# Moving group 1's transposes ahead of group 0's masks, group 4's transpose and group 5's loads ahead of the output weights, and tile 1's casts and masks to other steps

## The chip, the cores and the metric

The kernel runs on one core of one Trainium2 chip. The metric is the time of one execution on the device in microseconds (us), the median over the runs. Smaller is better. Profiled spans are some 1.7 us shorter than the time of the same run (236.5 for a run of 238.22).

With one core there is no second die to compare with. A run is called slow here only when it lies more than 1.5% above the fastest run of the same kernel, and ratios leave such runs out. The kernel before has such runs, and they turn out to matter, so below I give the whole spread too.

## The reference, cut to what matters

Causal linear attention with a decay per head, in blocks, then a gated feed-forward layer on its result:

```python
# per block of the sequence, state kv carried from block to block
intra = (q_b @ k_b^T) * Dmask          # scores, masked with the decay
out_b = intra @ v_b + (q_b * lam_pow) @ kv
kv    = lam_block * kv + (k_b * rev_pow)^T @ v_b
# then, on x = out of shape (3072, 512):
y = (silu(x @ w_gate) * (x @ w_val)) @ w_out     # d_ff = 1536
```

The kernel handles the 3072 rows as 12 groups of 256 rows, two groups to a tile of 512. A group is one batch element and two blocks of 128. Groups 0 to 3 are the first blocks of the four batch elements, groups 4 to 7 the next.

## The kernel before

TensorE's order is written by hand as a list of *steps* (one step is one chunk of 128 of the 1536 feed-forward columns: four gate matmuls, four value matmuls), and other work is attached behind a step with `at(step, ...)`. In the timelines of this case GpSimd and VectorE take their instructions in the order of the program. After the change, below, GpSimd's state sum starts at 68.45, just when the v scaling of another group ahead of it ends. In the profile before, VectorE's last mask of group 4 starts at 69.06, right behind a gating product for which VectorE sat idle 2.40 us, though the scores it masks had ended by 63.61. That is the point on which this case turns: an instruction attached early held up what stood behind it on its engine.

```python
def cast_scaled(g, eng=nc.vector):
    ...
    nc.scalar.copy(out=t[:, 0]..., in_=st[("kraw", g)]...)             # L238, ScalarE
    eng.tensor_tensor(out=t[:, 1]..., in0=st[("qraw", g)]..., in1=qd)  # L240, VectorE
    dma_transpose(g)                # L231: one DMA on the load queue, waits for both
def v_scale(g, eng, ...):           # L218, GpSimd
    eng.tensor_tensor(out=st[("vs", g)]..., in0=st[("v", g)]..., in1=rev)
def wo_cast():                      # L212, GpSimd: two of the twelve output-weight chunks
    nc.gpsimd.tensor_copy(out=o, in_=t)
def state(g):                       # L370, L374, L376, GpSimd
    ...                             # kvf = kvl + update; kvz = cast(kvf); kvl = kvf * lamblk
def inter(g, first):                # L386, TensorE: reads kvz
    for r in range(2): ...          # its second half needs state(g)
def ahead(g):
    upd(g)                          # update matmuls, their copy, state(g)
    scores(g)                       # L308; the masks follow on VectorE (L315)
```

The second tile's plan, cut to what moves (tile 1 holds groups 2 and 3; `s1a`: the steps on its first half, the rows of group 2; `s1b`: those on the rows of group 3; `s1c`: the last step, on all 512 rows. `core` is the rest of a group's attention: intra product, inter product and the copy of the result to `xt`):

```python
at(s0["11b"], load_group, 4, "v")
for c in range(0, FC, 2):
    at(s0["11b"], wo_piece, c, c + 2)          # six loads of output weights
...
at(s1a[9], core, 3, SPLIT)                     # intra + inter + evacuation of group 3
at(s1a[9], wo_cast); at(s1a[9], wo_cast)
at(s1a[10], cast_scaled, 4); at(s1a[10], load_group, 5)
...                                            # four more wo_cast at s1b[0], s1b[2]
at(s1b[8], ahead, 4); at(s1b[9], ffn_out, 0, 0)
at(s1b[10], cast_scaled, 5); at(s1b[10], v_scale, 5, nc.gpsimd)
at(s1b[10], load_group, 6)
at(s1b[10], core, 4); at(s1b[10], ffn_out, 0, 1)
at(s1c, ahead, 5); at(s1c, ffn_out, 0, 2); at(s1c, core, 5); at(s1c, ffn_out, 0, 3)
```

In the profile lines below, `qkt` is a group's transposed q and k, `ssb` its masked scores, `v_s` its scaled v, `kvf` and `kvz` the attention state, `woraw` and `wo_sb` the output weights as loaded and as cast, `xt` the attention result that the feed-forward part reads. On TensorE L308 is the scores, L338 the update, L401 the intra and L386 the inter product, L438 and L445 the gate and value matmuls, L460 the output blocks (two lines further down in e_warm from L386 on). "Start to start" means from the start of one group of matmuls to the start of the next; what lies beyond the usual spacing of the two is counted as a wait.

## Time and profile before

| | before |
|---|---|
| median of the first runs | 235.75 us (234.77 to 236.21) |
| the profiled run | 238.22 us, span 236.5 |
| TensorE busy | 224.0 us, 95% |
| waits of TensorE of some 1 us or more after the prologue | four, all between 50 and 96 us |

The median here is of the three runs known when the prediction was made; the fourth, 236.00, puts it at 235.88 further down. One line of this table deserves a second look before the prediction is read: the profiled run is 2.5 us longer than the median of the others. The prediction counts waits in that profile and takes them off the median.

On that profile's page one slice of TensorE's clock stands at 7 tenths: from 76.97 to 80.38, for 3.41 us, the granted clock is 0.50. Such a stretch is meant where a *window* at half clock is spoken of, in the recorded texts too.

### The profile page before, as it was taken

To read this page: it belongs to the slowest core of one execution; us is meant where nothing else is said; L and a number is where in the kernel's file an instruction comes from. 1 tells how busy PE (TensorE), PEld (TensorE's weight loads), DVE (VectorE), ACT (ScalarE), POOL (GpSimd) and SP (SyncE) were. 2 spreads that over 40 slices of the span, in tenths; PEclk is the share of its full clock that TensorE was granted. 3 is DMA by queue.
4 is the path that set the end of the run, shared out by engine and by line. 5 is a ranking of instruction groups with operands and counts; after the bars stand their busy time and mean duration, and the time that the engine had idled before them with its cause. 6 is when DMAs were issued, how large, how long until landed. Compare 5 with 4: busy or idle time off the path is not lost.

```text
span 236.5 us, 5408 instructions
## 1 busy us (share of the span) xinstructions
PE 224.0 (95%) x2215; PEld 122.6 (52%) x2228; DVE 105.0 (44%) x186; ACT 105.1 (44%) x203; POOL 80.0 (34%) x116
## 2 busy tenths in 40 slices
PE   7899999989986898999999999999999999999994
PEld 3566456868853444455454454454454444444443
DVE  5654887567553413546346245255263232232200
ACT  5878586646444053336254254263243344223311
POOL 4667775736992530836532032041020000000000
PEclk9999999999999799999999999999999999999999
DMA  6999999897945926777872924914101001101122
GB/s 201 345 336 362 358 314 312 214 375 252 231 139 139 261 91 170 234 186 217 209 237 72 295 79 71 309 69 101 44 35 44 37 10 46 44 3 44 44 89 89
DMA packets 71018, 39.66 MB, mean 168 GB/s; under 512 B 20178, under 2 KB 66514, under 8 KB 70994
## 3 DMA queue, kind: packets, MB, share of 16 engines
q1 hardware_dynamic: 66482, 32.64, 48.8%
q10 hardware_dynamic: 4512, 6.69, 8.1%
q8 instruction: 17, 0.28, 0.5%
q14 instruction: 7, 0.06, 0.1%
HBM read 28.31 MB, written 6.29 MB: 146 GB/s over the span
## 4 chain that ended last, share of the span: by engine, by line
PE 87%; DMA 6%; DVE 2%; ACT 2%; issue 1%; ACTq 0%; SPq 0%; DVEq 0%
PE bank L460 26%; PE bank L438 25%; PE bank L445 25%; DMA qkt<-qk 4%; PE bank L308 3%; PE bank L401 3%; PE bank L386 2%; DMA kraw<-in_k_dram 1%; DVE ssb L315 1%; PE bank L269 1%; PE bank L338 1%; PE bank L149 1%; ACT xt L412 0%; ACT sil L442 0%; DVE xt L412 0%
## 5 line engine op out<-in xcount | busy, mean ns | idle before, releaser
L448 DVE TENSOR_TENSOR h<-sil,bank 128x512 bf16<-128x512 bf16 (+1 forms) x86 | 51.2, 599 | 105.3 <-PE bank L445 95.7
L438 PE MATMUL bank<-xt,wg_sb 128*128 128x512 bf16 (+1 forms) x344 | 76.5, 345 | 1.6 <-DVE ssb L315 1.0
L445 PE MATMUL bank<-xt,wv_sb 128*128 128x512 bf16 (+1 forms) x344 | 76.3, 344 | 0.0
L442 ACT ACTIVATE sil<-bank 128x512 bf16<-128x512 f32 (+1 forms) x86 | 45.4, 530 | 49.2 <-PE bank L438 46.3
L460 PE MATMUL bank<-wo_sb,h 128*128 128x512 bf16 (+1 forms) x287 | 65.4, 373 | 1.0 <-issue 0.4
L445 PEld LDWEIGHTS <-wv_sb 128*128 128x128 bf16 x344 | 33.7, 98 | 28.8 <-issue 0.2
L438 PEld LDWEIGHTS <-wg_sb 128*128 128x128 bf16 x344 | 32.5, 98 | 29.6 <-issue 1.2
L460 PEld LDWEIGHTS <-h 128*128 128x128 bf16 x300 | 29.4, 99 | 33.2 <-issue 1.5
L462 ACT COPY osb<-bank 128x512 f32<-128x512 f32 (+1 forms) x24 | 13.9, 577 | 60.1 <-PE bank L460 60.1
L370 POOL TENSOR_TENSOR kvf<-kvl,ups 128x256 f32<-128x256 f32 x16 | 11.6, 728 | 67.3 <-ACT ups L360 66.7
L315 DVE TENSOR_TENSOR ssb<-bank,mask 128x512 bf16<-128x512 f32 x40 | 26.1, 685 | 7.7 <-PE bank L308 7.6
L218 POOL TENSOR_TENSOR v_s<-v,rev 128x1024 bf16<-128x1024 f32 (+1 forms) x14 | 23.8, 1704 | 9.9 <-DMA v<-in_v_dram 6.0
L412 ACT CAST xt<-bank 128x512 bf16<-128x512 f32 x21 | 14.4, 737 | 9.1 <-PE bank L401 7.8
L374 POOL CAST kvz<-kvf 64x256 bf16<-64x256 f32 x32 | 13.7, 427 | 1.7
L308 PE MATMUL bank<-qkt 64*64 64x128 bf16 x384 | 9.7, 234 | 4.1 <-DMA qkt<-qk 3.5
L240 DVE TENSOR_TENSOR qk<-qraw,qd 128x1024 bf16<-128x1024 f32 x8 | 11.6, 1455 | 0.0
L308 PEld LDWEIGHTS <-qkt 64*64 64x64 bf16 x384 | 6.9, 114 | 6.6 <-DMA qkt<-qk 3.7
L401 PE MATMUL bank<-ssb,v_s 64*64 64x128 bf16 x384 | 8.6, 227 | 1.1 <-DVE ssb L315 1.1
L238 ACT CAST qk<-kraw 128x1024 bf16<-128x1024 f32 x9 | 9.4, 1039 | 0.0
L212 POOL CAST wo_sb<-woraw 128x1024 bf16<-128x1024 f32 x6 | 6.9, 1159 | 7.0 <-DMA woraw<-in_moe_w_out_dram 7.0
L201 POOL CAST wv_sb<-wraw 128x512 bf16<-128x512 f32 (+1 forms) x9 | 6.8, 754 | 3.9 <-DMA wraw<-in_moe_w_val_dram 3.9
L401 PEld LDWEIGHTS <-v_s 64*64 64x64 bf16 x384 | 6.3, 111 | 3.3 <-issue 2.5
(57 smaller groups left out, 104.7 us busy)
## 6 DMA issues: line engine op xcount, KB each, us to landing
out_dram<-osb ACTq DMA_DIRECT2D x23, 256.0 KB, 2.1
kraw<-in_k_dram SPq DMA_DIRECT2D x10, 512.0 KB, 5.5
qraw<-in_q_dram SPq DMA_DIRECT2D x10, 512.0 KB, 6.0
v<-in_v_dram SPq DMA_DIRECT2D x10, 512.0 KB, 6.6
woraw<-in_moe_w_out_dram SPq DMA_DIRECT2D x6, 512.0 KB, 8.7
wraw<-in_moe_w_gate_dram SPq DMA_DIRECT2D x6, 256.0 KB, 5.5
wraw<-in_moe_w_val_dram SPq DMA_DIRECT2D x6, 256.0 KB, 5.0
wraw<-in_moe_w_gate_dram SPq DMA_DIRECT2D x3, 512.0 KB, 6.8
```

What stands on the lines that cost most here:

```text
L218: eng.tensor_tensor(out=st[("vs", g)][:, h0:h1], in0=st[("v", g)][:, h0:h1].rearrange("p h (s d) -> p h s d", s=2), in1=bap(rev, [[2, h1 - ...
L308: nc.tensor.matmul(sp[(c, h2)][b2 * M:b2 * M + M, n:n + BLK], tt[dp, 0, s, hp, b2 * M:b2 * M + M], tt[dp, 1, :, hp, b2 * M:b2 * M + M], st ...
L315: nc.vector.tensor_tensor(out=ssb[:, h2, 2 * c:2 * c + 2].rearrange("p a s n -> p a (s n)"), in0=sp[(c, h2)].rearrange("p (a x) -> p a x", ...
L374: nc.gpsimd.tensor_copy(out=kvz[b][(i + 1) % 2 if r else 2][dp, :, h2, :], in_=kv[dp])
L401: nc.tensor.matmul(op[r][h2 * 64:h2 * 64 + 64, hp * BLK:hp * BLK + BLK], v_s[ps, 2 * hp + h2, s], ssb[ps, h2, hp, s], start=((first or (i ...
L412: fns[r](out=xt[:, g % 2, :, r].rearrange("p h (m s) -> p h s m", s=2), in_=op[r].rearrange("p (h s m) -> p h s m", h=HP, s=2))
L438: nc.tensor.matmul(gp[:, 0:N], wg_sb[:, mc, fs], xt[:, b0 // 2:b1 // 2, mc].rearrange("p g b n -> p g (b n)"), start=(mc == 0), stop=(mc = ...
L442: nc.scalar.activation(sil[:, 0:N], gp[:, 0:N], AF.Silu)
L445: nc.tensor.matmul(vp[:, 0:N], wv_sb[:, mc, fs], xt[:, b0 // 2:b1 // 2, mc].rearrange("p g b n -> p g (b n)"), start=(mc == 0), stop=(mc = ...
L448: nc.vector.tensor_tensor(out=h_sb[:, fc, b0:b1].rearrange("p b n -> p (b n)"), in0=sil[:, 0:N], in1=vp[:, 0:N], op=ALU.mult)
L460: nc.tensor.matmul(ps, h_sb[:, fc, b], wo_sb[:, fc, c0:c1], start=(fc == 0), stop=(fc == FC - 1))
L462: fn(out=osb[:, c0:c1], in_=ps)
```

## The change

Its intent: have every DMA transpose and every load out before TensorE needs its result, and fill the latency of the prologue. The diff, cut to its core:

```diff
 # prologue (cut): two groups interleaved, more dummy matmuls
-    scores(0, (0,), 1)
+    scores(0, (0,), 3)
 ...
+    cast_half(1, 0, (POOLC, DVEC))          # group 1, ahead of group 0's masks
     run_later(2)
     upd_mm(0, up)
+    ring[0] = 4
+    pe_transpose(1, 0)                      # ahead of group 0's intra product
 ...
 # tile 1
-    for c in range(0, FC, 2):
-        at(s0["11b"], wo_piece, c, c + 2)
-    at(s1a[6], scores, 3)
-    at(s1a[9], core, 3, SPLIT)
-    at(s1a[10], cast_scaled, 4)
-    at(s1a[10], load_group, 5)
-    ... six wo_cast at s1a[9], s1b[0], s1b[2]; v_scale 4 at s1b[1]; state 3 at s1b[3]
-    at(s1b[8], ahead, 4)
-    at(s1b[9], ffn_out, 0, 0)
-    at(s1b[10], cast_scaled, 5); v_scale 5; load_group 6
+    at(s1a[3], cast_scaled, 4)
+    at(s1a[3], load_group, 5)
+    for c in range(0, FC, 2):
+        at(s1a[3], wo_piece, c, c + 2)      # now behind group 4's transpose and group 5
+    at(s1a[6], scores, 3, (0,))
+    at(s1a[7], scores, 3, (1,))
+    at(s1a[10], core, 3, SPLIT); v_scale 4; state 3
+    at(s1b[4], cast_scaled, 5); load_group 6
+    for j in (4, 5, 6):
+        at(s1b[j], wo_cast); at(s1b[j], wo_cast)
+    at(s1b[6], v_scale, 5, nc.gpsimd)
+    at(s1b[7], ahead, 4)                    # its state(4) now behind all of these on GpSimd
     at(s1b[10], core, 4)
+    s1c: ffn_out 0 0, ahead 5, ffn_out 0 1, ffn_out 0 2, core 5, cast_scaled 6, load_group 7, v_scale 6
```

More of the change, by code (lines that the diff above doesn't have):

```diff
@@ L491, in _body @@
     w_piece(4, 6)
-    cast_half(0, 0, (ACTC, DVEC))
+    cast_half(0, 0, (None, DVEC))
     nc.scalar.activation(cinvt, lnp, AF.Exp, scale=-float(BLK))
-    nc.scalar.activation(rev, rev, AF.Exp)
     qdec_table(0)
     qdec_table(1)
+    cast_half(0, 0, (ACTC, None))
+    nc.scalar.activation(rev, rev, AF.Exp)
+    nc.scalar.activation(qd, qd, AF.Exp)
+    nc.scalar.activation(cinv, ln_lam, AF.Exp, scale=-float(BLK))
+    nc.scalar.activation(lamblk, lnp, AF.Exp, scale=float(BLK))
     cast_half(0, 1, (None, DVEC))
@@ L508, in _body @@
     run_later(1)
-    scores(0, (1,), 2)
-    nc.scalar.activation(qd, qd, AF.Exp)
-    nc.scalar.activation(cinv, ln_lam, AF.Exp, scale=-float(BLK))
-    nc.scalar.activation(lamblk, lnp, AF.Exp, scale=float(BLK))
+    scores(0, (1,), 3)
     nc.scalar.preload_act_table_set("silu_and_others")
+    cast_half(1, 0, (POOLC, DVEC))
     run_later(2)
@@ L517, in _body @@
     upd_mm(0, up)
+    ring[0] = 4
+    pe_transpose(1, 0)
     upd_copy(0, (0,))
-    cast_half(1, 0, (POOLC, DVEC))
     cast_half(1, 1, (POOLC, DVEC))
+    ring[0] = 2
     st[("op", 0)] = [bank() for _ in range(2)]
-    warm_into(st[("op", 0)][0], 2)
+    warm_into(st[("op", 0)][0], 3)
     intra(0, True)
-    pe_transpose(1, 0)
-    inter(0, False)
-    pe_transpose(1, 1)
-    upd_copy(0, (1,))
     ring[0] = 4
     scores(1, (0,), 1)
-    scores(1, (1,), 2)
+    run_later(1)
+    ring[0] = 6
+    pe_transpose(1, 1)
+    inter(0, False)
+    run_later(1)
+    upd_copy(0, (1,))
+    ring[0] = 6
+    scores(1, (1,), 3)
     evac(0, (ACTC, None))
@@ L533, in _body @@
     v_scale(1, nc.gpsimd, H // 2, H)
-    run_later(4)
+    run_later(2)
     ring[0] = 0
@@ L607, in _body @@
     s1c = step(1, FC - 1)
-    at(s1a[6], scores, 3)
-    at(s1a[6], upd_mm, 3)
-    at(s1a[6], upd_copy, 3)
-    at(s1a[6], run_later, 2)
-    at(s1a[9], core, 3, SPLIT)
-    at(s1a[9], wo_cast)
-    at(s1a[9], wo_cast)
-    at(s1a[10], cast_scaled, 4)
-    at(s1a[10], load_group, 5)
-    at(s1b[0], wo_cast)
-    at(s1b[0], wo_cast)
-    at(s1b[1], v_scale, 4, nc.gpsimd)
-    at(s1b[2], wo_cast)
-    at(s1b[2], wo_cast)
-    at(s1b[3], state, 3)
-    at(s1b[8], ahead, 4)
-    at(s1b[9], ffn_out, 0, 0)
-    at(s1b[10], cast_scaled, 5)
-    at(s1b[10], v_scale, 5, nc.gpsimd)
-    at(s1b[10], load_group, 6)
+    at(s1a[3], cast_scaled, 4)
[4 more added lines that the diff above has]
+    at(s1a[7], scores, 3, (1,))
+    at(s1a[7], upd_mm, 3)
+    at(s1a[7], upd_copy, 3)
+    at(s1a[10], core, 3, SPLIT)
+    at(s1a[10], v_scale, 4, nc.gpsimd)
+    at(s1a[10], state, 3)
+    at(s1b[4], cast_scaled, 5)
+    at(s1b[4], load_group, 6)
+    for j in (4, 5, 6):
+        at(s1b[j], wo_cast)
+        at(s1b[j], wo_cast)
+    at(s1b[6], v_scale, 5, nc.gpsimd)
+    at(s1b[7], ahead, 4)
     at(s1b[10], core, 4)
-    at(s1b[10], ffn_out, 0, 1)
+    at(s1c, ffn_out, 0, 0)
     at(s1c, ahead, 5)
+    at(s1c, run_later, 3)
+    at(s1c, ffn_out, 0, 1)
     at(s1c, ffn_out, 0, 2)
     at(s1c, core, 5)
+    at(s1c, cast_scaled, 6)
+    at(s1c, load_group, 7)
+    at(s1c, v_scale, 6, nc.gpsimd)
     at(s1c, ffn_out, 0, 3)
@@ L638, in _body @@
         if t == 2:
-            at(sn[0], cast_scaled, 6)
-            at(sn[0], v_scale, 6, nc.gpsimd)
-            at(sn[0], load_group, 7)
             at(sn[2], ahead, 6)
```

## The prediction

> **What bounds the kernel now.** I read the page first, then the chain of waits in order of time, then the timelines of TensorE, GpSimd and the load queue where that chain leaves TensorE. The page and its slices:
>
> ```profile
> span 236.5 us, 5408 instructions
> ...
> PE 224.0 (95%) x2215; PEld 122.6 (52%) x2228; DVE 105.0 (44%) x186; ACT 105.1 (44%) x203; POOL 80.0 (34%) x116
> ...
> PEclk9999999999999799999999999999999999999999
> ...
> PE 87%; DMA 6%; DVE 2%; ACT 2%; issue 1%; ACTq 0%; SPq 0%; DVEq 0%
> ```
>
> TensorE sets the end: 95% busy, 87% of the chain. Nothing makes its matmuls cheaper here, so only its waits can be won, plus the slice where its clock fell to 7 tenths. After 100 us it is busy for 132.68 of 136.5 us (the view of stretches), so the waits lie before. The chain names two:
>
> ```profile
> 72.43 4.95 DMA qkt<-qk
> 77.43 1.07 PE bank L308 x30
> ...
> 89.67 5.38 DMA qkt<-qk
> 95.09 0.64 PE bank L308 x32
> ```
>
> The scores of groups 5 and 6 wait for a DMA transpose that was issued five microseconds before they needed it. The first also leaves TensorE at half speed: the same 32 matmuls take 1.07 us instead of 0.64. TensorE's timeline has the sizes (in brackets: idle time and what ended it):
>
> ```profile
> 51.86 0.60 PE L438 MATMUL bank<-xt,wg_sb 128*128 128x256 bf16 x4 [1.01 <-DVE ssb L315]
> ...
> 69.79 0.41 PE L401 MATMUL bank<-ssb,v_s 64*64 64x128 bf16 x15 [0.90 <-DVE ssb L315]
> ...
> 77.43 1.07 PE L308 MATMUL bank<-qkt 64*64 64x128 bf16 x32 [2.42 <-DMA qkt<-qk]
> ...
> 95.09 0.64 PE L308 MATMUL bank<-qkt 64*64 64x128 bf16 x32 [1.09 <-DMA qkt<-qk]
> ```
>
> Measured from start to start, beyond the usual spacing, they cost: masks of group 3, 1.35 (1.18 + 0.17); masks of group 4, 1.45 (1.10 + 0.35); transpose of group 5, 2.6 plus 1.5 for some 3 us at half clock; transpose of group 6, 1.3. Together 8.2 us, all in tile 1 and at the start of tile 2.
>
> GpSimd is in program order and feeds the attention state:
>
> ```profile
> 60.70 1.03 POOL L212 CAST wo_sb<-woraw 128x1024 bf16<-128x1024 f32 x1
> ...
> 64.66 0.72 POOL L370 TENSOR_TENSOR kvf<-kvl,ups 128x256 f32<-128x256 f32 x1
> 65.44 0.83 POOL L374 CAST kvz<-kvf 64x256 bf16<-64x256 f32 x2
> ```
>
> The last cast of the output weights ends at 61.7; group 4's state is ready at 66.3, and the inter-block product that reads it starts at 67.9. The margin is 1.6 us, and the weights had been requested since 45.25:
>
> ```profile
> 42.88 1.70 SPq L231 DMA_TRANSPOSE qkt<-qk  x1
> 44.63 0.57 SPq L92 DMA_DIRECT2D v<-in_v_dram  x1
> 45.25 3.69 SPq L207 DMA_DIRECT2D woraw<-in_moe_w_out_dram  x6
> ```
>
> The prologue (TensorE's first gate matmul is at 17.3) is latency-bound:
>
> ```profile
> 11.28 0.98 PE bank L401 x30
> ...
> 15.39 1.29 DVE ssb L315 x2
> ```
>
> Group 1's masks end at 16.7, and ScalarE's evacuation of group 0 ends at 17.25. Both end just before the first gate matmul, so shortening one alone gains nothing.
>
> [...] the loads issued behind the transpose of 89.67 land at 96.8, 98.3 and 99.8.
>
> **The change part by part** (minus is a gain; times on the scale of the kernel before).
>
> *Prologue, −0.6.* Group 1's first transposes and casts go ahead of group 0's last masks and intra product; scores and masks of the two groups interleave; four small exponentials move to where ScalarE waits for data; dummy matmuls go from 1+2+2+1+2 to 3+3+3+1+3. VectorE still does eight masks (0.62 each) and the same casts. Followed engine by engine with the row durations: at full clock from about 9 us on, group 1's second transposes end near 12.3 instead of 13.3, the state copies at 13.8, ScalarE's last evacuation of group 0 at 16.0, gate matmuls at 16.0: −1.3. If the clock rises only at 12.1 as now, the eight extra transposes (0.86 at half clock) and three dummies (0.63) stand before the intra product, and the evacuation ends at 17.3: 0. I take about half. Weight casts allow it: the second piece ends at 16.8 on GpSimd, needed at 16.9.
>
> *Scores and core of group 3, +1.0.* The scores come in two halves, one step apart, their masks behind each step's gating product. The second step after reuses the first half's banks: a wait of 0.75; two steps on, the second half's: 0.6. And the core moves from the step before last of the first half-tile to the last one, directly ahead of the step that reads its result: 0.95 for one evacuation (0.73 plus two handovers), which a step of 0.87 covers now. 2.3 against 1.35.
>
> *Transposes of groups 5 and 6, −2.6 −1.5 −1.3.* Group 5's casts and transpose come about six 0.87 us steps earlier, group 6's ahead of the last output block of tile 0. With some 5 us to landing, both are in before their scores. The half-clock stretch goes too.
>
> *Group 4's state, −1.45 +3.6 +1.5.* This is the new wait I expect. The six output-weight loads now stand behind group 4's transpose and group 5's three loads on one queue. VectorE's gating product of the fourth step ends at 46.05; scaling q takes 1.45 (row L240); the transpose goes out at 47.5. Behind a transpose the v load has landed 10.1 to 10.2 us after the transpose's issue (89.67 to 99.83): 57.7. The weights land 1.28 apart ((58.68 − 54.84) / 3): the sixth at 57.7 + 6 × 1.28 = 65.4. GpSimd then has, in order: its cast 1.04, v scaling of group 5 (now ahead) 1.90, state sum 0.72, two casts 0.83: 69.9. TensorE gets there at 48.0 (end of the seventh step) + 15 steps × 0.875 + 0.67 scores + 0.35 update + 0.8 core of group 3 + 0.85 update and scores of group 4 + 2.3 waits + 0.2 = 66.3. Wait: 3.6, and after it one window at half clock, 1.5. It swallows the old mask wait.
>
> *Output blocks* only change places. Sum: −0.6 + 1.0 − 2.6 − 1.5 − 1.3 − 1.45 + 3.6 + 1.5 = −1.35, so 235.75 − 1.35 = 234.4 us.
>
> **Rivals.** (a) The output weights arrive in time, as the order of the plan intends. For it: without a transpose ahead the six landed within 13.4 us of the first issue, and TensorE has 21 us from the scaling to the core. Against it: 10 us of transpose and loads come first, and 4.5 us of GpSimd work follow. It would need 3.6 us less; then the sum is −6.45, about 229.3. (b) The wait is longer, since v of group 4 is still landing when the transpose starts: the transpose of 57.15, with weights still in flight, had its v load in after 11.3 instead of 10.2. One more microsecond and a second window at half clock: 236 to 237. (c) The prologue gains nothing or loses a little to the dummies at half clock: 235. With (b), 237.5.
>
> **Range and chances.** The chance of 2% (231.0 or less) hangs on (a), in whole or most part. I trust the queue's order and GpSimd's order, and the two sums (69.9 and 66.3) are good to about a microsecond each, so (a) gets 0.16. Slower by 2% (240.5) would need two misses: 0.06. Range 231.0 to 237.5.
>
> **What would show it.** Right: no wait for qkt near the scores of groups 5 and 6; at the inter product of group 4 (L386 in the kernel before) TensorE or its weight load idle 2.5 to 4.5 us, released by GpSimd's kvz cast; the last output-weight cast ending near 66 less the prologue's gain; half clock just after; waits for masks and for xt around group 3's core; the first gate matmul between 16.0 and 17.3. Wrong: the last weight cast before 62, or no idle time at group 4's core; then the change is worth over 2%. New waits after 100 us would also break it.

## The result, and the profile after

The changed kernel took 239.19 us in the median (238.33 to 239.81, 4 runs), the kernel before 235.88 (4 runs). The ratio is 1.0146, 95% interval 1.0098 to 1.0195. A ratio is the mean time of one kernel's fast runs over that of the other's of the same rounds, so it is not quite the ratio of the medians. The change makes the kernel slower by about 1.5%; the prediction said 234.4, with 231.0 to 237.5 as its range. It was wrong, and in direction too.

The changed kernel's page, the lines that answer to those shown of before:

```profile
span 236.6 us, 5423 instructions
...
PE 224.3 (95%) x2233; PEld 121.6 (51%) x2233; DVE 102.9 (44%) x186; ACT 105.5 (45%) x203; POOL 82.1 (35%) x116
...
PEclk9999999999997999999999999999999999999999
...
PE 82%; DMA 6%; SPq 4%; POOL 2%; DVE 2%; ACT 1%; issue 1%; DVEq 0%; POOLq 0%; ACTq 0%
```

The span is 236.6 against 236.5: by the two profiles nothing changed, while the runs differ by 3.3 us. One of the two profiles must be of an untypical run. There is again one slice at reduced clock, one earlier than before. TensorE's timeline (start, duration, in brackets the idle time and what ended it):

```profile
49.87 0.60 PE L438 MATMUL bank<-xt,wg_sb 128*128 128x256 bf16 x4 [0.58 <-DVE ssb L315]
...
52.25 0.60 PE L438 MATMUL bank<-xt,wg_sb 128*128 128x256 bf16 x4 [0.31 <-DVE ssb L315]
...
55.16 0.60 PE L438 MATMUL bank<-xt,wg_sb 128*128 128x256 bf16 x4 [0.82 <-ACT xt L412]
...
70.09 0.40 PE L386 MATMUL bank<-qkt,kvz 128*128 128x128 bf16 x4 [3.82 <-POOL kvz L374]
70.42 0.64 PE L401 MATMUL bank<-ssb,v_s 64*64 64x128 bf16 x32
70.99 1.67 PE L438 MATMUL bank<-xt,wg_sb 128*128 128x512 bf16 x4
```

The scores of groups 5 and 6 no longer wait. In their place TensorE stands idle 3.82 us at group 4's inter product, until GpSimd has cast the state, and the gate matmuls after it take 1.67 us for four instead of 1.03. The chain of waits leads from there back through GpSimd to the last two loads of output weights (start, length, what):

```profile
55.51 8.71 DMA woraw<-in_moe_w_out_dram
64.22 0.05 issue
64.28 1.04 POOL wo_sb L212
...
65.55 1.04 POOL wo_sb L212
66.59 1.86 POOL v_s L218
68.45 0.69 POOL kvf L370
...
69.20 0.39 POOL kvz L374
69.59 0.04 issue
69.63 0.41 POOL kvz L374
70.04 0.05 issue
70.09 0.40 PE bank L386 x4
```

This is the new wait that the prediction described: the sixth weight load landed at 65.50 (foreseen 65.4), the state was ready at 70.04 (69.9), TensorE came at 66.1 (66.3). That the single times agree so closely is partly luck. The prediction's are on the scale of the kernel before, and this profile's first gate matmul is 0.8 us earlier (16.5 against 17.3); put on one scale, all three came 0.6 to 0.9 us later than foreseen, and the errors nearly cancel in the difference (a wait of 4.0 us for 3.6). So the mechanism of the loss was right, and the question is which gain did not come.

### The profile page after: what moved, and what is told of

It reads as the page before. It is cut to its first block, busy times and chain, and to the rows that moved or that the text cites. A ratio compares the mean times of both kernels' runs of the same rounds, so it can differ in the third digit from the quotient of the medians.

```text
span 236.6 us, 5423 instructions
## 1 busy us (share of the span) xinstructions
PE 224.3 (95%) x2233; PEld 121.6 (51%) x2233; DVE 102.9 (44%) x186; ACT 105.5 (45%) x203; POOL 82.1 (35%) x116
## 4 chain that ended last, share of the span: by engine, by line
PE 82%; DMA 6%; SPq 4%; POOL 2%; DVE 2%; ACT 1%; issue 1%; DVEq 0%; POOLq 0%; ACTq 0%
PE bank L460 27%; PE bank L438 24%; PE bank L445 23%; DMA woraw<-in_moe_w_out_dram 4%; PE bank L401 2%; SPq L92 2%; DMA qraw<-in_q_dram 2%; PE bank L308 2%; PE bank L386 2%; SPq L207 1%; PE bank L338 1%; POOL wo_sb L212 1%; ACT xt L412 1%; POOL v_s L218 1%; PE bank L269 1%
## 5 line engine op out<-in xcount | busy, mean ns | idle before, releaser
L445 PE MATMUL bank<-xt,wv_sb 128*128 128x512 bf16 (+1 forms) x344 | 77.2, 347 | 0.0
L374 POOL CAST kvz<-kvf 64x256 bf16<-64x256 f32 x32 | 14.4, 451 | 1.7
L240 DVE TENSOR_TENSOR qk<-qraw,qd 128x1024 bf16<-128x1024 f32 x8 | 10.3, 1291 | 0.0
L386 PE MATMUL bank<-qkt,kvz 128*128 128x128 bf16 x80 | 6.6, 219 | 3.8 <-POOL kvz L374 3.8
L376 POOL TENSOR_TENSOR kvl<-kvf,lamblk 128x256 f32<-128x256 f32 x12 | 9.1, 756 | 1.0
L308 PE MATMUL bank<-qkt 64*64 64x128 bf16 x384 | 8.8, 219 | 0.4 <-DVE qkt L280 0.4
L386 PEld LDWEIGHTS <-kvz 128*128 128x128 bf16 x80 | 5.2, 98 | 6.1 <-POOL kvz L374 4.0
```

The lines of the kernel that those rows point to most:

```text
L308: nc.tensor.matmul(sp[(c, h2)][b2 * M:b2 * M + M, n:n + BLK], tt[dp, 0, s, hp, b2 * M:b2 * M + M], tt[dp, 1, :, hp, b2 * M:b2 * M + M], st ...
L374: nc.gpsimd.tensor_copy(out=kvz[b][(i + 1) % 2 if r else 2][dp, :, h2, :], in_=kv[dp])
L386: nc.tensor.matmul(op[r][:, hp * BLK:hp * BLK + BLK], kvz[b][2 if r else i % 2][:, hp], tt[:, 1, :, hp, r * M:r * M + M], start=(first and ...
L445: nc.tensor.matmul(vp[:, 0:N], wv_sb[:, mc, fs], xt[:, b0 // 2:b1 // 2, mc].rearrange("p g b n -> p g (b n)"), start=(mc == 0), stop=(mc = ...
```

## The experiments

Twelve kernels ran. Each run of a call is compared with runs of the kernel before on the same chip.

### Is it real, and which half does it? (four kernels, one call)

**e_before**: no edit.

> The kernel before once more, unchanged. The profiled execution of it was 238.22 us, its other runs 235.88 in the median, so the trace that the prediction was counted from may be of a slow execution. Theory A (the trace is typical): this profile again has some 2.4 us of wait for the transpose of group 5, a half-clock stretch after it, and a span of 236 to 237. Theory B (the trace was of a long execution): a span near 234, and a shorter wait or no half-clock stretch in tile 1. Ratio to the kernel before 1.00 in both.

Measured: 235.64 us (233.56 to 239.20, 23 runs), ratio 1.0003. The profile was again of a long run, 238.86 us. But the runs show two kinds: of the 43 runs of the kernel before in this call, 8 lie at 238.79 or above, the others at 237.72 or below. Over all four timed calls, 34 of 138 runs lie at 237.9 or above (mean 238.8), the other 104 average 235.6. Below, the first kind are called long runs and the others usual ones. Both profiles that I had were of long runs. So Theory B was right as to the kind of run; the second half of it, a shorter wait in a usual run, had to wait for a profile of one (e_look).

**e_after**: no edit.

> The changed kernel once more, unchanged. If the 1.5% is real: ratio 1.010 to 1.020 again, with a wait of 3.5 to 4.5 us for group 4's state at L386 and the half-clock stretch behind it. If it was an accident of the runs: ratio 1.000 to 1.005, as the two traces (236.6 and 236.5) say.

Measured: 239.59 us (238.19 to 239.91, 6 runs), ratio 1.016 (1.0105 to 1.0215). The loss is real. Every run lies above 238, so this kernel has no quick kind. Its profile has a wait of 3.86 us (start to start, beyond the usual spacing) at group 4's state, and the clock stays low longer than in the first profile. In the view of stretches (from:to and length in us; busy time and number of instructions of PE, PEld, DVE, ACT and POOL; then the granted clock, here 0.82 and 0.64, the DMA share and GB/s):

```profile
66.00:71.00 5.00, 1.31 (x14) 0.85 (x11) 2.12 (x5) 0.38 (x1) 4.60 (x6) 0.82 0.96 254
71.00:78.00 7.00, 7.00 (x54) 3.36 (x55) 0.69 (x1) 1.92 (x3) 2.74 (x5) 0.64 0.34 102
78.00:106.00 28.00, 28.00 (x286) 13.54 (x285) 11.52 (x16) 11.63 (x21) 13.95 (x18) 1.00 0.53 147
```

The trace's clock record puts the drop at 69.22 and the return at 76.05, 6.83 us, where the first profile has 71.26 to 74.67, 3.41 us. So half clock came with the wait for one window in the first profile and for two, one behind the other, in this one.

**e_pro**: the new prologue with the old tile 1.

```diff
 (kernel before)
-    prologue as before
+    prologue as in the change
```

> The prologue of the change alone, tile 1 as before. Prediction: 0.6 us less than before (ratio 0.9975); the two traces put the first gate matmul at 16.5 instead of 17.3, so 0.8 less (0.9966) if nothing gives it back. Rival: the early start is given back at a load or a transpose in tile 0 or 1, ratio 1.000; or the prologue is what costs the 3.3 us, ratio above 1.01.

Measured: 236.29 us (22 runs), ratio 0.9997 (0.9965 to 1.0029). The predicted 0.9975 lies inside the interval, and so does no gain at all. The long runs are there as before (7 of 22). The rival that the prologue itself costs the 3.3 us is out.

**e_tile1**: the old prologue with the new tile 1.

```diff
 (changed kernel)
-    prologue as in the change
+    prologue as before
```

> The tile 1 part alone, prologue as before. The prediction's terms for it: -0.75 us (235.0 of 235.75, ratio 0.997). From the trace of the changed kernel with its 4.0 us at group 4's state: about 0 (ratio 1.000). If tile 1 is what costs the 3.3 us: ratio near 1.017.

Measured: 240.17 us (6 runs), ratio 1.0202 (1.0149 to 1.0256). Tile 1 carries the whole loss. Its profile has a wait of 5.06 us at group 4's state and again 6.8 us at half clock (71.34 to 78.16 in the clock record).

### What the wait costs, and what the clock adds (four kernels, one call)

**e_state**: in the changed kernel, only GpSimd's order is turned round.

```diff
-    for j in (4, 5, 6):
+    for j in (4, 5):
         at(s1b[j], wo_cast)
         at(s1b[j], wo_cast)
-    at(s1b[6], v_scale, 5, nc.gpsimd)
     at(s1b[7], ahead, 4)
+    at(s1b[7], wo_cast)
+    at(s1b[7], wo_cast)
+    at(s1b[7], v_scale, 5, nc.gpsimd)
```

> The changed kernel with one order turned round on GpSimd: four weight casts, then group 4's state, then the last two weight casts and group 5's v scaling. Loads, transposes and TensorE's order as in the change. Theory (group 4's state behind the weight casts costs the time, the wait of 3.9 to 5.1 us and the one or two half-clock windows behind it): no wait at group 4's inter product over 0.5 us, no half-clock record in tile 1, about 5.5 us less than the change: 233.5 to 234.5, ratio to before 0.99 to 0.995. Rival (what costs is the new order of loads, or the waits around group 3's core): the wait moves to the first output block or to the v scaling of group 5, and the time stays over 237.

Measured: 234.89 us (233.32 to 237.01, 15 runs), ratio 0.9962 (0.9932 to 0.9993): 4.7 us less than e_after of the call before (239.59 − 234.89; the ratios to the kernel before, 1.016 and 0.9962, say the same), from the place of three instructions. GpSimd's timeline shows the state between the fourth and the fifth weight cast:

```profile
61.63 3.77 POOL L212 CAST wo_sb<-woraw 128x1024 bf16<-128x1024 f32 x3 [0.28 <-DMA woraw<-in_moe_w_out_dram]
65.37 0.72 POOL L370 TENSOR_TENSOR kvf<-kvl,ups 128x256 f32<-128x256 f32 x1
66.15 0.83 POOL L374 CAST kvz<-kvf 64x256 bf16<-64x256 f32 x2
...
70.01 2.02 POOL L212 CAST wo_sb<-woraw 128x1024 bf16<-128x1024 f32 x2
71.99 1.90 POOL L218 TENSOR_TENSOR v_s<-v,rev 128x1024 bf16<-128x1024 f32 x1
```

and TensorE's, what is left of the wait, now for a mask, and a small new one for the v scaling that was put off:

```profile
68.00 0.38 PE L386 MATMUL bank<-qkt,kvz 128*128 128x128 bf16 x4 [0.54 <-DVE ssb L315]
...
73.94 0.45 PE L338 MATMUL bank<-v_s,qk 64*64 64x64 bf16 x32 [0.56 <-POOL v_s L218]
```

The theory holds: the output weights' casts ahead of the state on GpSimd are what costs the time. The median lies 0.4 us above the expected band, and the gain is 4.7 us where 5.5 was expected; the expectation had left out the two small waits. One of the 15 runs, 237.01 us at a mean clock of 0.993, was left out of the ratio as slow; one window at half clock would give that mean (1 − 0.5 × 3.41 / 235 = 0.993), but no profile shows one.

**e_warm**: the changed kernel with dummy matmuls in the wait.

```diff
 def inter(g, first):
     ...
+        if g == 4 and r == 1:
+            warm_into(banks[ring[0] % 8], 16, 512)
```

> The changed kernel with 16 dummy matmuls of 512 columns (3.5 us at full clock) between the two halves of group 4's inter product, into a free bank: they fill the wait and end before group 4's state is there. Wait unchanged in length, clock kept. If the half clock after the wait is part of the cost: no half-clock record, 1.5 to 3 us less than the change (236.5 to 238). If only the wait counts: 239.5 as the change.

Measured: 237.59 us (236.23 to 239.86, 22 runs), 2.0 us less than e_after (239.59 − 237.59), ratio to before 1.0084 (1.0059 to 1.0109). The dummies end before the state comes, so the wait as a whole is as long as before:

```profile
66.15 3.62 PE L149 MATMUL bank<-warm 128*128 128x512 bf16 x16
70.01 0.40 PE L388 MATMUL bank<-qkt,kvz 128*128 128x128 bf16 x4 [0.25 <-POOL kvz L374]
70.34 0.64 PE L403 MATMUL bank<-ssb,v_s 64*64 64x128 bf16 x32
70.91 1.04 PE L440 MATMUL bank<-xt,wg_sb 128*128 128x512 bf16 x4
```

The four gate matmuls behind it take 1.04 us instead of 1.67. Of the loss, about 2 us is so put down to the half clock that follows the wait (1.8 us by the two ratios to the kernel before, which is the fairer measure, since e_after ran in another call on another chip).

**e_bwarm**: the kernel before with dummies inside the wait for group 5's transpose.

```diff
     def ahead(g):
         upd(g)
-        scores(g)
+        scores(g, (0, 1), 10 if g == 5 else 0)      # ten dummies of 256 columns
```

> The kernel before with ten dummy matmuls of 256 columns (1.07 us at full clock) ahead of the scores of group 5, inside the wait for their transpose. 8 of 43 runs of the kernel before lie at 238.8 or above, and both its profiles, with a half-clock record at 77 us, are of that kind. If the half clock after this wait makes those long runs: none above 238, median unchanged near 235.5. If something else makes them: still about one run in five at 239.

Measured: 235.87 us (234.74 to 238.41, 14 runs), one run of 14 above 237.9 instead of one in four. Ratio 1.0016. Expected were none, so this is a miss by one run, and a weak test: 13 of 57 runs of the kernel before in the same call are long, and at that rate 14 runs would have one or none about one time in seven. It suggests that the half clock behind that wait belongs to the long runs and doesn't show it. Nor does it say why the wait is long in some runs only.

**e_state_core**: e_state with the core of group 3 one step earlier.

```diff
-    at(s1a[10], core, 3, SPLIT)
+    at(s1a[9], core, 3, SPLIT)
```

> As the first run of this call, and the core of group 3 one step earlier, so that a step stands between it and the step that reads its result. Masks are then the last to come. Expected 0.4 to 0.9 us less than the first run of this call (the 0.98 us wait for xt goes, part of it comes back as a wait for the masks): 233 to 234. If the placement of the core does not matter: equal to the first run.

Measured: 234.96 us (19 runs), ratio 0.9974; no difference from e_state. A miss: the 0.98 us wait for xt goes, but group 3's masks take its place (0.47 and 0.58 us in its profile, start to start).

### A usual run of the kernel before, and a better order (three kernels, one call)

**e_look**: the kernel before, one profile.

> The kernel before, one look, for a profile of a run of the usual kind (235 to 236 us). Expected there, if the half-clock stretch is what sets the long runs apart: a wait for group 5's transpose of 1.2 to 1.6 us instead of 2.6 to 2.8, and no half-clock record before the end. If the profile is again of 238 us or more: the same as before, and nothing new.

Measured: 234.67 us, a usual run at last. It has no wait for group 5's transpose at all:

```profile
75.15 0.45 PE L338 MATMUL bank<-v_s,qk 64*64 64x64 bf16 x32
75.47 0.64 PE L308 MATMUL bank<-qkt 64*64 64x128 bf16 x32
76.04 2.76 PE L460 MATMUL bank<-wo_sb,h 128*128 128x512 bf16 x12
```

The update matmuls are followed by the scores after 0.32 us and at full clock, where the first profile had 2.42 us idle and half clock. The expectation (1.2 to 1.6 us) was too high for this run. The transpose was issued at 71.69 and landed at 75.42; in the first profile it was issued at 72.43 and landed at 77.38. Counted from TensorE's update matmuls (75.15 and 74.56), the issue was 1.3 us later in the long run and the landing took 1.2 us more (4.95 instead of 3.73). The later issue starts at the instruction that the transpose waits for. The usual run:

```profile
70.24 1.31 DVE L240 TENSOR_TENSOR qk<-qraw,qd 128x1024 bf16<-128x1024 f32 x1
...
70.43 2.88 POOL L218 TENSOR_TENSOR v_s<-v,rev 128x1024 bf16<-128x1024 f32 x1
```

and the first profile, the long run:

```profile
69.66 2.64 DVE L240 TENSOR_TENSOR qk<-qraw,qd 128x1024 bf16<-128x1024 f32 x1
...
69.32 1.90 POOL L218 TENSOR_TENSOR v_s<-v,rev 128x1024 bf16<-128x1024 f32 x1
```

In both traces the two engines run side by side on this stretch, and whichever starts first takes its usual time (1.31 us for VectorE's scaling of q, 1.90 for GpSimd's scaling of v) while the other is held up, by 1.0 us in e_look (2.88 for 1.90) and by 1.3 to 1.4 in the long run (2.64 for 1.22 to 1.31). In the long run VectorE's instruction ends at 72.30, which is 1.08 us after GpSimd's end at 71.22. In e_look it's GpSimd's that is stretched, and nobody waits for that one.

But e_look is one usual run, and two more on record are of the other order. In e_pro (235.18 us; new prologue, old tile 1) GpSimd starts first too:

```profile
69.12 2.21 DVE L240 TENSOR_TENSOR qk<-qraw,qd 128x1024 bf16<-128x1024 f32 x1
...
68.34 1.90 POOL L218 TENSOR_TENSOR v_s<-v,rev 128x1024 bf16<-128x1024 f32 x1
...
71.46 3.98 DMA qkt<-qk
75.44 0.04 issue
75.49 0.64 PE bank L308 x32
```

TensorE sat idle 1.02 us there (1.2 beyond the usual spacing) and kept its full clock (0.64 us for the 32 matmuls). In e_bwarm (235.69 us; the kernel before with dummies in the wait) GpSimd is first as well, VectorE's scaling takes 2.02, and the transpose lands after 3.72 us. So GpSimd's being first does not by itself make a long run. In these two the transpose was issued 2.6 and 2.75 us ahead of TensorE's update matmuls, in the two long runs 2.1 and 1.9 us ahead, and in the long runs the landing took 4.9 us. In the long runs ScalarE had issued the store of an output block 1.1 and 0.9 us after the transpose; in the usual ones that gap was 1.55 us (e_pro) or more. That a late transpose meets this store and is slowed by it would fit, but no run isolates it.

**e_mix**: the kernel before with only the transposes' order changed, and its weight loads left alone.

```diff
+    at(s1a[3], cast_scaled, 4)
+    at(s1a[3], load_group, 5)         # was s1a[10]; stays behind the weight loads
-    at(s1b[9], ffn_out, 0, 0)
-    at(s1b[10], cast_scaled, 5)
+    at(s1b[9], cast_scaled, 5)
+    at(s1b[9], load_group, 6)
+    at(s1b[9], ffn_out, 0, 0)
     at(s1c, core, 5)
+    at(s1c, cast_scaled, 6)           # with load_group 7 and v_scale 6; were at step 0 of tile 2
```

> The kernel before, prologue and output-weight loads as they are, with only these moves: group 4's casts and transpose and group 5's loads seven steps earlier (behind the weight loads in the queue), group 5's casts and transpose ahead of the first output block, group 6's casts and transpose ahead of the last output block of tile 0. Theory: both waits for transposes go (1.2 and 1.3 us in a run without half clock) and no long runs remain, since nothing stops TensorE for over 1.3 us; the weights still arrive early, so group 4's state stays on time. Median 233.2 to 233.8, ratio 0.988 to 0.992, highest run under 237. Rival: group 4's transpose, now queued behind the weights, lands too late for its scores, or the casts delay a mask, and the time stays at 235 to 236.

Measured: 233.14 us (232.38 to 233.53, 6 runs), ratio 0.9866 (0.9821 to 0.9911). It beats both kernels, and no run is a long one, though six runs are few for a kind that comes one time in four. The waits that TensorE's timeline still records between 44 and 90 us:

```profile
47.56 0.64 PE L308 MATMUL bank<-qkt 64*64 64x128 bf16 x32 [0.65 <-DMA qkt<-qk]
51.31 0.60 PE L438 MATMUL bank<-xt,wg_sb 128*128 128x256 bf16 x4 [1.01 <-DVE ssb L315]
69.26 0.41 PE L401 MATMUL bank<-ssb,v_s 64*64 64x128 bf16 x15 [0.91 <-DVE ssb L315]
```

Groups 5 and 6 don't wait, and group 4's state is on time since the weights still come first.

**e_mix_pro**: the same tile 1 with the new prologue.

```diff
 (e_mix)
-    prologue as before
+    prologue as in the change
```

> The same tile 1 with the prologue of the change. If the prologue's 0.8 us lead at the first gate matmul is real [...]: 0.5 to 0.9 us less than the first run of this call. If it is given back later (a transpose or a weight load that does not come earlier): equal within 0.2.

Measured: 233.85 us (232.85 to 235.62, 6 runs), ratio 0.9893 (0.9841 to 0.9945). A miss: no gain from the prologue. Its profile, of the 235.62 us run, has 2.5 us of wait for group 3's transpose, which was issued at 43.56 and landed at 50.18 (in e_pro, with the same prologue, 42.34 and 46.83); why is open. Whether the 0.7 us between the two medians is real, six runs each don't settle.

### Who starts first (one kernel, one call)

**e_vdve**: the kernel before with group 5's v scaling on VectorE, behind q's, so that the two no longer run side by side.

```diff
-    at(s1b[10], v_scale, 5, nc.gpsimd)
+    at(s1b[10], v_scale, 5, nc.vector)
```

> The kernel before with one instruction on another engine: group 5's v scaling on VectorE, behind q's scaling, instead of on GpSimd beside it. In the two profiles of long runs GpSimd's v scaling had started 0.1 to 0.3 us before VectorE's scaling of q, which then took 2.64 and 2.85 us; in the profile of a usual run VectorE had started 0.2 us earlier, took 1.31, and GpSimd took 2.88 instead of 1.90. Theory (who starts first decides whether group 5's transpose is late, and that makes the long runs): scaling of q 1.2 to 1.4 us, wait for the transpose under 0.5 us, no runs above 238, median 235 or a little under. Rival (the long runs come from the clock's window alone or from the landing of the transpose): still one run in four or five above 238.

Measured: 234.54 us (233.74 to 235.22, 22 runs), ratio 0.9957 (0.9934 to 0.9979), and that is against the usual runs of the kernel before alone. The long kind is gone: none of 22 runs lies above 235.3, while 9 of the 27 runs of the kernel before in the same call lie at 238.3 or above. VectorE's two scalings, one after the other:

```profile
69.63 1.22 DVE L240 TENSOR_TENSOR qk<-qraw,qd 128x1024 bf16<-128x1024 f32 x1
70.76 1.22 DVE L218 TENSOR_TENSOR v_s<-v,rev 128x1024 bf16<-128x1024 f32 x1
```

So the overlap of the two scalings is a cause of the long runs: without it the transpose is issued 3.55 us ahead of the update matmuls, lands in time, and the long runs go. The chain in the two long profiles is: GpSimd starts first, the scaling of q takes twice as long (2.64 and 2.85 us), the transpose goes out late and lands late, TensorE sits idle 2.42 and 2.60 us, the clock drops to half for one window of 3.41 us. What makes this chain end in a long run in some executions and in a wait of 1.2 us at full clock in others (e_pro), the landing above all, is not shown.

## Why the prediction was wrong

| step of the prediction | predicted, us | what the runs showed |
|---|---|---|
| prologue | −0.6 | alone 0.9997 of before, so 0 with ±0.8 |
| scores and core of group 3 | +1.0 | waits 0.64 + 0.17 + 0.47 + 0.17 + 0.98 = 2.43, against 1.35: +1.1 |
| transpose of group 5, wait | −2.6 | in usual runs 0 (e_look) and −1.2 (e_pro) |
| the half clock after it | −1.5 | 0 in both usual runs |
| transpose of group 6 | −1.3 | −1.1 (1.08 in the usual run) |
| group 4's state: old mask wait, new wait, half clock | −1.45 +3.6 +1.5 | −1.1, +4.0 (3.9 and 5.1 in two more profiles), +1.7 (half of 3.41) to 2.0 (e_warm) |

**The step that failed** is "Transposes of groups 5 and 6, −2.6 −1.5 −1.3", in its first two terms. The mechanism was right in that the wait is gone after the change; but the wait that it removed was of the one profiled run, not of the runs whose median it was taken from. That profile was of a 238.22 us run. In the usual run of e_look (234.67) neither the wait nor the half clock is there, and in that of e_pro (235.18) the wait is 1.2 us and the half clock is not there. I set 4.1 us of gain against a median that contained, as far as these profiles show, at most about 1.2 us of that loss. Two signs were there beforehand: a profiled run 2.5 us above the median, and, in the profile itself, one scaling of q of 2.64 us where the median of the eight is 1.22 (the 1.45 that the prediction takes from row L240 is their mean, this one included). Taking the two terms out moves the prediction from 234.4 to 238.5, or to 237.3 if 1.2 us of the wait is kept, and the median was 239.2.

**The new wait** was predicted with its place, its releaser and its length (3.6 us against 4.0 in the first profile), and e_state shows that it is the cause: taking it away gives back 4.7 us. What was mis-sized there is the half clock behind it. I allowed one window; two of the three profiles have two (6.8 us at half clock), and e_warm puts the clock's share at 1.8 to 2.0 us, against 1.5. One reading in support of rival (a) was wrong as well: the six loads that landed within 13.4 us did have a transpose ahead of them, that of 42.88 in the lines shown, which landed at 47.22.

**The prologue** did start the feed-forward part earlier in the profiles, 16.5 against 17.3, but the step took one pair of runs for the rule. The profiles of this study put the first gate matmul at 16.5 to 16.8 with the new prologue, and at 15.9, 16.8, 17.3 and 17.7 to 17.9 with the old one. The 15.9 (e_mix) is the run in which the clock rose at 4.7 us, the 16.8 (e_vdve) the one in which it rose at 10.9; in the later ones it rose between 12.1 and 13.5 (in the profile before at 12.1: the prologue's transposes are 107 ns apart at 8 us and 56 ns after 12.2). With the new prologue it rose between 5.0 and 9.0. So in these profiles the new prologue evens out the start; alone it brings no measured gain. Part of a lead can be lost again at group 3's transpose, which TensorE waits for 0.8 to 0.9 us in the profiles of e_after and e_state and 2.3 in that of e_mix_pro (idle time), but also 0.65 in that of e_mix, with the old prologue.

**Group 3** came out as predicted, with the waits where they were expected (mask, mask, xt). e_state_core shows that the last of them can't be won by itself: the masks come due instead.

**The rivals.** (a), the weights in time, didn't happen; its 0.16 was the whole chance for "faster". (b) named the right direction, a longer wait with a second window at half clock, and gave it 236 to 237. Even so it carried the same 4.1 us. (c), no gain from the prologue, is what e_pro shows.

With the measured sizes the sum is 0 + 1.1 − 1.1 − 1.1 + 4.0 + 1.7 to 2.0 = +4.6 to +4.9, counted from a usual run without a wait for group 5. From the 234.67 us of e_look to the 239.59 us of e_after it is 4.9; from the mean of the usual runs (235.6) to the median of the first runs (239.19) 3.6. What separates these was not taken apart; a wait of up to 1.2 us for group 5 in some usual runs (e_pro) and the moment at which the clock rose in the prologue (4.7 to 13.5 us in the profiles) are candidates.

## What to carry to other kernels

Before you take a wait off a median, check that the profiled run is one of the runs of that median: compare its time with the spread of the others, and take a second profile if it stands out. When a load is moved ahead of another on one queue, follow the one that was pushed back (here the sixth weight load, landed at 65.50 instead of 58.68) through everything that stands behind it on the engine that consumes it; here two more weight casts and a v scaling in front of the attention state (e_state) cost more than two late transposes. And when two executions of the same program differ by a per cent on an undisturbed chip, look for two instructions that start within a microsecond of each other and hold each other up; here they started 0.1 to 1.0 us apart, one of them took 0.8 to 1.6 us longer than usual, and separating them (e_vdve) took away the long runs.

## What the traces showed of clock, overlap and transposes

- The clock dropped to half at waits with 2.42 and 2.60 us of idle time in both profiles of long runs (in the first at 76.97, when TensorE had been idle for 2.0 us) and not at one of 2.32 us (e_mix_pro). It stayed low for 3.41 us there, and with the waits of 3.9 to 5.1 us for group 4's state for 3.4 or 6.8 us.
- VectorE's scaling of q and GpSimd's of v held each other up: for group 5, the scaling of q took 1.22 us alone (e_vdve), 1.31 when first and 2.02 to 2.85 when second; the scaling of v 1.90 when first and 2.88 when second. The order of start changed from run to run of one kernel: GpSimd was first in the first profile and in e_before, VectorE in e_look. 34 of 138 runs of the kernel before were 3.3 us longer on average than the others, and with the two scalings kept apart none of 22 was.
- A DMA transpose from issue to landing took 3.7 to 5.4 us in the kernel before with nothing ahead of it in the queue, and up to 12.9 us behind the six weight loads (e_mix_pro). The third 512 KB load behind it landed 10.0 to 10.9 us after the transpose's issue in the first profile, and 9.6 to 11.8 over all profiles, again with nothing ahead.
